# The lower half of the second network's first group moves from VectorE to GpSimd, and the token numbers of all units are turned on the third bank

## The chip, the cores and the metric

The kernel runs on one core of one Trainium2 chip. The metric is device time in microseconds (us), lower is better. A core has five engines with a queue each: TensorE (PE, its weight loads are PEld), VectorE (DVE), ScalarE (ACT), GpSimd (POOL) and SyncE (SP, which here only issues transfers). They meet through semaphores alone. PE writes into eight PSUM banks; DVE and ACT read those, and everything else that is spoken of lies in SBUF.

## The reference

Three steps follow each other, all in float32. Only the third is touched in its order of work, and the second in one detail:

```python
x = _attn_ref(q, k, v)            # banded attention, 2 x 768 tokens of 512
x = _moe_ref(x, w_gate, w1, w2)   # one expert of eight for each token, capacity 384
h = x @ w_in                      # 1536 x 512 by 512 x 2048
g = np.where(h > 0, h, np.exp(np.minimum(h, 0)) - 1)
out = g @ w_out                   # 1536 x 2048 by 2048 x 512
```

## The kernel before

Products are made in a fast 32-bit matmul form from halves: each float32 operand is rounded to an upper half (`h` in a name), and the rest is the lower half (`l`), subtracted from the operand. A product is then three matmuls: upper by upper, lower by upper, upper by lower.

**Experts.** The routed tokens are worked in units of 384 tokens of one expert. At the start of a unit `split_x` (L246) turns the unit's rows: first a small matmul (L250) turns the token numbers into a corner of a PSUM bank, ACT copies them out (L251, tile `it`), and then the four quarters of the rows are transposed into banks 0, 5, 6 and 7 in turn (L255, three transposes each), rounded by ACT (L256) and their lower halves subtracted by DVE (L257). In the first unit the token numbers go to the third of the banks listed, in the later ones to the second, bank 5. A bank that still has to be read isn't written, so that transposes into the bank of the token numbers wait for L251. Here a first unit and two later ones run.

**Second network.** The 1536 rows are worked in four groups of 384. `group(g)` (L1432) goes through 16 tiles f of 128 features. In each:

- PE makes the 12 matmuls of `hidden` (L241) into one of four PSUM banks in rotation;
- ACT makes three activations of it (L1450 to L1452);
- DVE makes four dependent instructions (L1465 to L1468) that turn these into the activated block x; the last one reads PSUM and one SBUF operand, the other three read two SBUF operands;
- the block is halved into `hh` and `hl`, tiles of a ring of four (HH): in group 0 ACT rounds the block of the tile before (`round_g`, L1425) and DVE subtracts its lower half (`rest_g`, L1429); in the later groups DVE does both (L1474, L1429);
- PE multiplies with w_out, three tiles late (LAG): `second_2` (L1401) makes nine matmuls for tile f - 3, and among its first three stand one that reads the lower half of w_out and one that reads `hl`.

In group 0 both weight matrices are halved on the way, in pieces of two tiles: `split_a2` for w_in and `split_b2` for w_out, ACT rounding and DVE subtracting (L1381). Also there, DVE finishes the last conversion of w_out (L419, L422, L412, tiles 3 to 5) and four subtractions for the next group's rows (L1361, tiles 6 to 12). The order on each engine is the order in which the code is written (the schedule is made by hand), so `rest_g(f - 1)` stands on DVE behind tile f's four instructions and, at odd f, behind `split_b2`. POOL has nothing to do in group 0; its next work there is the scattered put of group 0's rows (L1413) in group 1.

Of the kernel before, what the change touches and what calls it, by code (L numbers as in the profile page):

```python
# [9 lines left out]
F32 = mybir.dt.float32  # L10
# [6 lines left out]
ALU = mybir.AluOpType  # L17
# [11 lines left out]
P = 128  # L29
# [6 lines left out]
SLOT = 384  # L36
NS = SLOT // P
# [57 lines left out]
def moe_chain_kernel(  # L95
# [14 lines left out]
    nc = tc.nc  # L110
# [47 lines left out]
    at, _ = nc.bump_sbuf(4 * KD * FF)  # L158
# [10 lines left out]
    at, _ = nc.bump_sbuf(4 * FF // P * DM)  # L169
# [57 lines left out]
    XROW0 = wout[:, 0:4, :].rearrange("p a d -> p (a d)")[:, 0 : NS * ROW].rearrange("p (s d) -> p s d", s=NS)  # L227
# [18 lines left out]
    def split_x(xrow, hps, it):  # L246

        xh, xl = XS1
        at = hps[2 if xrow is XROW0 else 1][0:NS, SLOT : SLOT + P]
        nc.tensor.matmul(at, xrow[:, :, DM], ident, start=True, stop=True)  # L250
        nc.scalar.copy(IT[it], at)  # L251
        for kk in range(KD):
            xp = hps[kk % len(hps)][:, 0:SLOT]
            for s in range(NS):
                nc.tensor.transpose(xp[:, s * P : (s + 1) * P], xrow[:, s, kk * P : (kk + 1) * P], ident)  # L255
            nc.scalar.copy(xh[:, kk, :], xp)  # L256
            nc.vector.tensor_tensor(xl[:, kk, :], xp, xh[:, kk, :].bitcast(F32), op=ALU.subtract)  # L257
            yield
# [111 lines left out]
    def conv_load(i, after=()):  # L370
        half = NCHUNK // 2
        for n in range(2):
            if i < half:
                part, kk = divmod(i + n, KD)
                src = w_in[kk * P : (kk + 1) * P, part * CE : (part + 1) * CE]
            else:
                src = w_out[(i + n - half) * P : (i + n - half + 1) * P, :]
            ld = nc.sync.dma_start(raw_pair(i)[:, n * CE : (n + 1) * CE], src).ins
            for rows in after if n == 0 else ():
                tc.add_manual_dep(  # L380
                    ld,
                    rows.name,
                    mybir.DependencyInfo(mybir.DependencyClass.Sync, mybir.DependencyReason.DATA),
                    reason="the first unit's rows go first",
                )
# [49 lines left out]
    with ExitStack() as att:  # L435
# [549 lines left out]
        for n in range(NST - 1):  # L985
            at = lambda lag: steps[n - lag] if 0 <= n - lag < NST else None
# [35 lines left out]
        def counts():  # L1022
# [87 lines left out]
            op=ALU.mult,  # L1110
# [36 lines left out]
    def listed(n, j):  # L1147
        return lists_i[:, n * MAXU + j : n * MAXU + j + 1]
# [5 lines left out]
    def hidden(wa, jj, xa):  # L1154
        hp = new_hp()
        for _ in layer1(hp, wa, jj, xa):
            pass
        return hp
# [40 lines left out]
    def prologue(j, n):  # L1199

        if n == 0:
            split_a(0, W1_RAW[0])
        elif n == 1:
            for _ in split_x(XROW, HP[1:] + HP[:1], j % 2):
                pass

    def branch_ahead(label, hint):

        engines = [e.engine for e in (nc.tensor, nc.vector, nc.scalar, nc.gpsimd, nc.sync)]
        tc.mark_branch_hint_location(label, hint=hint, engines=engines)  # L1210
# [142 lines left out]
    def load_y(g, at):  # L1353
        nc.sync.dma_start(YR, ydT[:, ds(at, SLOT)].rearrange("(k p) n -> p k n", p=P))
        nc.sync.dma_start(IDT[g % 3], ids[ds(at, SLOT), :].rearrange("(s p) o -> p (s o)", p=P))

    def split_y(g, parts):
        yh, yl = YS[g % 2]
        for kk in parts:
            nc.scalar.copy(yh[:, kk, :], YR[:, kk, :])  # L1360
            nc.vector.tensor_tensor(yl[:, kk, :], YR[:, kk, :], yh[:, kk, :].bitcast(F32), op=ALU.subtract)  # L1361
# [21 lines left out]
    def split_a2(c):  # L1383
        split_2(AW[c], half_part(IN, c))

    def split_b2(c):
        split_2(BW[c], OUT[c])
# [4 lines left out]
    RINGS = [HF + slots[0:2], slots[2:4]]  # L1392
# [3 lines left out]
    def second_2(f, s):  # L1396
        c, jj = divmod(f, 2)
        cols = slice(s * P, (s + 1) * P)
        ga, wb = HH[f % 4], BW[c]
        for n, (a, b) in enumerate(((0, 0), (0, 1), (1, 0))):  # L1400
            nc.tensor.matmul(  # L1401
                ACC[s],
                ga[a][:, cols],
                wb[b][:, jj, :],
                start=(f == n == 0),
                stop=(f == NF2 - 1 and n == 2),
            )

    def take_out(g, s):
        nc.scalar.copy(OBS[(NS * g + s) % len(OBS)], ACC[s])  # L1410

    def put_out(g, s):
        put = nc.gpsimd.indirect_dma_start(  # L1413
            out,
            bass.IndirectOffsetOnAxis(ap=IDT[g % 3][:, s : s + 1], axis=0),
            OBS[(NS * g + s) % len(OBS)],
            None,
            bounds_check=NT - 1,
            oob_is_err=False,
        ).ins  # L1420
        tc.declare_no_dep(put, group="out", reason="no two rows have one token")
        tc.add_to_no_dep_group("out", put)

    def round_g(f):
        nc.scalar.copy(HH[f % 4][0], RINGS[0][f % 4])  # L1425

    def rest_g(f):
        gh, gl = HH[f % 4]
        nc.vector.tensor_tensor(gl, RINGS[0][f % 4], gh.bitcast(F32), op=ALU.subtract)  # L1429

    def group(g, tail):

        more = g + 1 < NG
        if g == 0:
            conv_load(NCHUNK - CONV_LATE)
        for f in range(NF2):
            c, jj = divmod(f, 2)
            if g == f == 0:
                split_b2(0)
            if g == 0 and f < LAG:  # L1440
                tail(f)
            if more and f == HINT_AT:
                branch_ahead(f"groups{g}", n_rows > (g + 1) * SLOT)
            hp = hidden(AW[c], jj, YS[g % 2])
            if g == 0 and jj == 0 and c + 1 < NC2:
                split_a2(c + 1)


            x, z = RINGS[0][f % 4], RINGS[1][f % 2]
            nc.scalar.activation(x, hp, AF.Relu, scale=-1.0)  # L1450
            nc.scalar.activation(z, x, AF.Tanh, scale=-0.5)  # L1451
            nc.scalar.activation(x, x, AF.Exp, scale=-1.0)  # L1452
            if f >= LAG:
                for s in range(NS):
                    second_2(f - LAG, s)
            elif g:
                for s in range(NS):
                    second_2(NF2 - LAG + f, s)
                    if f == LAG - 1:
                        take_out(g - 1, s)  # L1460
            if more and f == (0 if g else LAG - 1):
                load_y(g + 1, nc.sync.value_load(listed(NLIST - 1, 3 + g), min_val=0, max_val=NT - SLOT))
            if g == 0 and f:
                round_g(f - 1)
            nc.vector.scalar_tensor_tensor(z, x, 1.0, z, op0=ALU.add, op1=ALU.mult)  # L1465
            nc.vector.tensor_tensor(x, z, x, op=ALU.subtract)  # L1466
            nc.vector.scalar_tensor_tensor(x, x, 3.0, z, op0=ALU.add, op1=ALU.mult)  # L1467
            nc.vector.scalar_tensor_tensor(x, x, 0.5, hp, op0=ALU.mult, op1=ALU.max)  # L1468
            if g == 0 and jj and c:
                split_b2(c)  # L1470
            if g == 0 and f:
                rest_g(f - 1)
            if g or f == NF2 - 1:
                nc.vector.tensor_copy(HH[f % 4][0], x)  # L1474
                rest_g(f)
            if g == 0:
                lo, hi = (min(max(n - LATE_FROM, 0) * LATE_STEPS, len(late)) for n in (f, f + 1))
                for step in late[lo:hi]:
                    step()
            if g and f in PUTS:  # L1480
                put_out(g - 1, PUTS.index(f))
            if g == 0 and 2 <= f < 2 + NG:

                m = f - 2
                nc.sync.dma_start(
                    out[m * SLOT : (m + 1) * SLOT, :].rearrange("(s p) d -> p s d", p=P),
                    fill_row[:, 0:DM].unsqueeze(1).to_broadcast([P, NS, DM]),
                )
            if more and 6 <= f < 14 and jj == 0:
                split_y(g + 1, [(f - 6) // 2])  # L1490
# [14 lines left out]
    def groups(g, tail=None):  # L1505
        group(g, tail)
        if g + 1 < NG:
            with tc.If(n_rows > (g + 1) * SLOT, label=f"groups{g}") as more:
                groups(g + 1)
            with more.Else():  # L1510
                last_products(g)
        else:
            last_products(g)
# [4 lines left out]
    with tc.If(n_rows <= 2 * SLOT, label="rows"):  # L1518


        at = nc.sync.value_load(last_i[:, 0:1], min_val=0, max_val=NT)
# [52 lines left out]
```

## Time and profile before

| | us |
|---|---|
| median of three timed runs | 414.65 (414.61 to 416.39) |
| the profiled execution, its own time | 416.77 |
| its span from the first to the last instruction | 414.8 |
| PE busy | 396.7 (96%) |
| DVE busy | 335.1 (81%) |
| ACT busy | 236.2 (57%) |
| POOL busy | 65.0 (16%) |

The span has three stretches: attention and routing up to about 110 us, the expert units to about 205 us, and the four groups of the second network from there to the end, at about 67 us each. The granted clock of TensorE is 0.996 of full speed as a mean.

In the timeline's rows below the columns are start, duration (both us), engine, line, operation, output and inputs, shape, count, and in brackets the idle time just before and what ended it. Rows of four matmuls of a kind are merged into one row, whose start is that of the first.

### The profile page before, as it was taken

How to read it: one execution, taken by the hardware profiler on the slowest of the kernel's cores; microseconds unless marked ns; L12 is line 12 of the kernel's file. 1: busy time of each engine (PE TensorE's matmuls, PEld its weight loads, DVE VectorE, ACT ScalarE, POOL GpSimd, SP SyncE). 2: the span in 40 equal slices, each digit the busy share in tenths (PEclk: the TensorE clock that was granted, in tenths of full speed). 3: DMA queues.
4: the chain of work that ended last, by engine and by line, in shares of the span. 5: the costliest groups of instructions: out<-in, count | busy, mean ns of one | idle time of the engine just before them, and what ended most of it. 6: DMA issues, size and time to landing. Idle time of an engine off the chain costs nothing.

```text
span 414.8 us, 7899 instructions
## 1 busy us (share of the span) xinstructions
PE 396.7 (96%) x2736; PEld 346.8 (84%) x2736; DVE 335.1 (81%) x675; ACT 236.2 (57%) x588; POOL 65.0 (16%) x127
## 2 busy tenths in 40 slices
PE   7898999989999999999999999999999999999994
PEld 4586677668998989999889789998989898989883
DVE  6779788677589989878889999997788777778871
ACT  4887698673565738437586677635343425253421
POOL 5134876553100000000000000002000003000002
PEclk9999999999999999999999999999999999999998
DMA  8999998699576787995477000202000201000002
GB/s 258 274 278 270 283 286 255 184 348 316 186 250 226 245 292 260 349 285 186 158 241 304 0 2 0 78 0 77 0 0 2 77 2 50 26 2 0 2 2 77
DMA packets 33691, 63.60 MB, mean 153 GB/s; under 512 B 5302, under 2 KB 16191, under 8 KB 33642
## 3 DMA queue, kind: packets, MB, share of 16 engines
q1 hardware_dynamic: 31962, 58.28, 45.3%
q0 software_dynamic: 1680, 4.73, 3.1%
q8 instruction: 23, 0.38, 0.4%
q14 instruction: 26, 0.21, 0.1%
HBM read 50.19 MB, written 13.40 MB: 153 GB/s over the span
## 4 chain that ended last, share of the span: by engine, by line
PE 27%; issue 14%; DVE 6%; DMA 1%; POOL 1%; ACT 1%; another core or an unknown queue 0%; POOLq 0%; DVEq 0%
PE bank L241 14%; PE bank L1401 14%; DVE xrow L1465 1%; DMA raw<-in_moe_w_out_dram 1%; DVE win_r L1381 1%; DVE hl L1429 1%; POOL out_dram L1413 1%; DVE wout_r L1381 1%; DVE cst L1467 1%; DVE cst L1466 1%; DVE xrow L1466 0%; DVE xrow L1467 0%; DVE wout L412 0%; DVE wout L422 0%; ACT xrow L1451 0%
## 5 line engine op out<-in xcount | busy, mean ns | idle before, releaser
L1401 PE MATMUL bank<-wout_r,hh 128*128 128x512 f32 x144 | 56.5, 393 | 0.0
L640 ACT ACTIVATE ex<-bank,nm 128x120 f32<-128x120 f32 x96 | 33.5, 369 | 8.1 <-DVE nm L627 7.7
L1450 ACT ACTIVATE cst<-bank 128x384 f32<-128x384 f32 x24 | 11.8, 490 | 38.8 <-PE bank L241 38.8
L1450 ACT ACTIVATE xrow<-bank 128x384 f32<-128x384 f32 x24 | 11.8, 490 | 38.4 <-PE bank L241 38.2
L1401 PEld LDWEIGHTS bank<-wout_r,hh 128*128 128x128 f32 x144 | 27.1, 188 | 4.6 <-DVE wout_r L1381 0.3
L1413 POOL DMA_INDIRECT out_dram<-ysb,idt x3 | 2.9, 976 | 175.9 <-DVE xrow L1466 175.3
L1401 PE MATMUL bank<-w2raw_r,hl 128*128 128x512 f32 x72 | 28.8, 399 | 1.2 <-DVE hl L1429 1.2
L1401 PE MATMUL bank<-w2raw_r,hh 128*128 128x512 f32 x72 | 28.2, 392 | 0.0
L241 PE MATMUL bank<-yh,win_r 128*128 128x384 f32 x128 | 27.0, 338 | 0.0
L615 PE MATMUL bank<-kw,half 128*64 128x120 f32 x384 | 24.8, 271 | 1.9 <-DMA half<-in_q_dram 1.1
L615 PEld LDWEIGHTS bank<-kw,half 128*64 128x64 f32 x384 | 19.8, 136 | 6.2 <-issue 3.8
L1413 POOL DMA_INDIRECT out_dram<-raw,idt x6 | 6.1, 1024 | 119.3 <-ACT raw L1410 118.1
L241 PE MATMUL bank<-xh,wal 128*128 128x384 f32 x104 | 22.9, 341 | 0.9 <-DVE wal L234 0.9
L241 PEld LDWEIGHTS bank<-yh,win_r 128*128 128x128 f32 x128 | 22.8, 188 | 0.3
L1465 DVE SCALAR_TENSOR_TENSOR xrow<-xrow 128x384 f32<-128x384 f32 x24 | 13.4, 557 | 9.3 <-ACT xrow L1452 8.6
L275 PE MATMUL bank<-hh,wbh_r 128*128 128x384 f32 x96 | 20.8, 337 | 0.0
L275 PE MATMUL bank<-hl,wbh_r 128*128 128x384 f32 x96 | 20.6, 336 | 0.0
L640 ACT ACTIVATION_READ_ACCUMULATOR ex<-bank,nm 128x1 f32 x96 | 20.5, 214 | 0.0
L1465 DVE SCALAR_TENSOR_TENSOR xrow<-cst,xrow 128x384 f32<-128x384 f32 x24 | 13.3, 556 | 8.5 <-ACT cst L1452 8.5
L241 PEld LDWEIGHTS bank<-xh,wal 128*128 128x128 f32 x104 | 18.1, 188 | 2.5 <-DVE wal L234 2.2
L1401 PEld LDWEIGHTS bank<-w2raw_r,hl 128*128 128x128 f32 x72 | 13.5, 188 | 5.5 <-DVE hl L1429 2.6
L269 ACT ACTIVATE xrow<-xrow,gate 128x512 f32<-128x512 f32 x9 | 6.5, 722 | 20.1 <-DVE gate L264 15.9
(287 smaller groups left out, 1116.1 us busy)
## 6 DMA issues: line engine op xcount, KB each, us to landing
raw<-in_moe_w_out_dram SPq DMA_DIRECT2D x16, 512.0 KB
w1raw<-in_moe_w_dram SPq DMA_DIRECT2D x12, 512.0 KB
w2raw<-in_moe_w_dram SPq DMA_DIRECT2D x12, 512.0 KB
raw<-in_moe_w_in_dram SPq DMA_DIRECT2D x10, 512.0 KB
half<-in_q_dram SPq DMA_DIRECT2D x24, 128.0 KB
w2raw<-in_v_dram SPq DMA_DIRECT2D x6, 512.0 KB
rows<-in_moe_w_in_dram SPq DMA_DIRECT2D x6, 512.0 KB
yr<-ydT SPq DMA_DIRECT2D x4, 768.0 KB
```

What stands on the lines that cost most here:

```text
L241: nc.tensor.matmul(hp, wa[a][:, kk, cols], xa[b][:, kk, :], start=(n == kk == 0), stop=(n == 2 and kk == KD - 1))
L269: nc.scalar.activation(xrow[:, s, 0:DM], xrow[:, s, 0:DM], AF.Copy, scale=GATE[:, s : s + 1])
L275: nc.tensor.matmul(ACC[d][:, 0:SLOT], wb[a][:, jj, d * P : (d + 1) * P], hb[b], start=(f == 0 and n == 0), stop=(f == NF1 - 1 and n == 2),)
L615: nc.tensor.matmul(sp[cols, u, :], qts[i][:, g, u, cols], kws[i][:, g, u, j, :], start=True, stop=True)
L640: nc.scalar.activation(ex[:, u, :], sp[:, u, :], AF.Exp, bias=nm[:, u : u + 1], accum_out=dens[i][:, g, u])
L1381: nc.vector.tensor_tensor(lo, src, hi.bitcast(F32), op=ALU.subtract)
L1401: nc.tensor.matmul(ACC[s], ga[a][:, cols], wb[b][:, jj, :], start=(f == n == 0), stop=(f == NF2 - 1 and n == 2),)
L1413: put = nc.gpsimd.indirect_dma_start(out, bass.IndirectOffsetOnAxis(ap=IDT[g % 3][:, s : s + 1], axis=0), OBS[(NS * g + s) % len(OBS)], No ...
L1429: nc.vector.tensor_tensor(gl, RINGS[0][f % 4], gh.bitcast(F32), op=ALU.subtract)
L1450: nc.scalar.activation(x, hp, AF.Relu, scale=-1.0)
L1465: nc.vector.scalar_tensor_tensor(z, x, 1.0, z, op0=ALU.add, op1=ALU.mult)
L1466: nc.vector.tensor_tensor(x, z, x, op=ALU.subtract)
```

## The change

```diff
@@ split_x
-        at = hps[2 if xrow is XROW0 else 1][0:NS, SLOT : SLOT + P]
+        at = hps[2][0:NS, SLOT : SLOT + P]
@@
-    def rest_g(f):
+    def rest_g(f, engine=nc.vector):
         gh, gl = HH[f % 4]
-        nc.vector.tensor_tensor(gl, RINGS[0][f % 4], gh.bitcast(F32), op=ALU.subtract)
+        engine.tensor_tensor(gl, RINGS[0][f % 4], gh.bitcast(F32), op=ALU.subtract)
@@ group
             if g == 0 and f:
-                rest_g(f - 1)
+                rest_g(f - 1, nc.gpsimd)
```

Fifteen subtractions, those of tiles 0 to 14 of group 0, go from DVE's queue to POOL's. The one of tile 15 and those of the later groups stay on DVE. In the later units the token numbers are turned into bank 6 instead of bank 5.

On DVE, in group 0 at tile 1 (`cst` and `xrow` are the rings of blocks, `hl0` the lower half of tile 0, `win1` the second quarter of w_in), a line with a minus stands only in the kernel before:

```order
 L1467 SCALAR_TENSOR_TENSOR cst_66<-cst_66,xrow_1892 128x384
 L1468 SCALAR_TENSOR_TENSOR cst_66<-cst_66,bank5_89 128x384
-L1429 TENSOR_TENSOR hl0_152<-cst_66,hh0_151 128x384
 L1381 TENSOR_TENSOR win1_r_97<-win1_96,wal1_143 128x4x256
 L1465 SCALAR_TENSOR_TENSOR xrow_1892<-xrow_1892 128x384
```

The subtraction is gone, and the next piece of w_in follows the tile's last instruction at once. On POOL, from the branch into the second network on:

```order
 L1518 COMPARE_AND_BRANCH
 L1518 UNCONDITIONAL_BRANCH x2
-L1210 REGISTER_ALU
-L1570 BRANCH_PREFETCH_HINT
+L1429 TENSOR_TENSOR hl0_152<-cst_66,hh0_151 128x384
+L1429 TENSOR_TENSOR hl1_154<-cst_66,hh1_153 128x384
+L1429 TENSOR_TENSOR hl2_156<-xrow_1892,hh2_155 128x384
+L1429 TENSOR_TENSOR hl3_1901<-xrow_1892,hh3_1900 128x384
```

Eleven more like these follow, around the branch hint, and then the puts of group 1 as before; between the fifteen POOL has no other work. On PE, at the start of a later unit (`xrow` are the unit's rows, `cst` holds the identity):

```order
 L275 MATMUL bank4_88<-hh1_153,wbh0_r_145 128x384
-L250 MATMUL bank5_89<-cst_66,xrow_1892 3x128
+L250 MATMUL bank6_90<-cst_66,xrow_1892 3x128
 L255 MATMUL bank0_84<-cst_66,xrow_1892 128x128 x3
 L255 MATMUL bank5_89<-cst_66,xrow_1892 128x128 x3
```

The matmul keeps its place and writes the bank that the transposes reach third instead of second.

## Rows read from the trace of the kernel before

**Rows 1.** Busy time in two stretches of group 0: PE, PEld, DVE, ACT, POOL, clock, DMA
```profile
210.48:237.65 27.17, 26.02 (x130) 22.84 (x128) 26.44 (x43) 18.64 (x35) 0.00 (x0) 1.00 0.47 165
243.01:259.34 16.33, 16.33 (x84) 14.87 (x83) 15.91 (x27) 12.03 (x22) 0.00 (x0) 1.00 0.00 1
```

**Rows 2.** Chain that ended last, by time: start, us, what
```profile
237.09 0.56 DVE hl L1429
...
237.70 1.90 PE bank L1401 x7
...
348.54 2.10 PE bank L241 x12
```

**Rows 3.** Timeline of PE: first matmuls of tiles 3, 4, 8, 10, 12; one of tile 15
```profile
212.19 0.85 PE L241 MATMUL bank<-yh,wah 128*128 128x384 f32 x4
...
217.30 0.87 PE L241 MATMUL bank<-yh,wal 128*128 128x384 f32 x4
...
234.43 0.87 PE L241 MATMUL bank<-yh,w1raw_r 128*128 128x384 f32 x4
...
243.74 0.87 PE L241 MATMUL bank<-yh,w1raw_r 128*128 128x384 f32 x4
...
252.11 0.87 PE L241 MATMUL bank<-yh,w1raw_r 128*128 128x384 f32 x4
...
266.97 0.39 PE L1401 MATMUL bank<-wout_r,hh 128*128 128x512 f32 x1
```

**Rows 4.** Timeline of DVE: two tiles of group 0, and a later piece of w_out
```profile
241.40 0.55 DVE L1429 TENSOR_TENSOR hl<-xrow,hh 128x384 fp32r<-128x384 f32 x1
241.87 1.22 DVE L1381 TENSOR_TENSOR win_r<-win,w1raw_r 128x1024 fp32r<-128x1024 f32 x1
243.01 0.55 DVE L1465 SCALAR_TENSOR_TENSOR xrow<-cst,xrow 128x384 f32<-128x384 f32 x1
...
251.17 0.55 DVE L1465 SCALAR_TENSOR_TENSOR xrow<-xrow 128x384 f32<-128x384 f32 x1
...
264.77 1.22 DVE L1381 TENSOR_TENSOR wout_r<-wout,wbh_r 128x1024 fp32r<-128x1024 f32 x1
```

**Rows 5.** Instructions of POOL by line: count, shortest/median/longest ns, first and last start
```profile
L567 POOL TENSOR_TENSOR w2raw<-w2raw x12: 453/460/589, 35.2 to 43.6; 128x128 f32<-128x128 f32 x12
L926 POOL TENSOR_TENSOR wal<-w1raw,wah_r x4: 717/724/742, 61.2 to 74.2; 128x256 fp32r<-128x256 f32 x4
L764 POOL TENSOR_SCALAR idx<-row,ob x9: 294/299/1279, 38.2 to 93.8; 128x1 uint32<-128x1 f32 x9
```

**Rows 6.** Timeline of DVE and POOL where both read SBUF, or one alone
```profile
33.26 0.29 DVE L514 TENSOR_SCALAR kw<-rows 64x384 f32<-64x384 f32 x1
...
40.57 0.32 DVE L514 TENSOR_SCALAR kw<-rows 64x320 f32<-64x320 f32 x1
...
42.61 0.54 POOL L567 TENSOR_TENSOR w2raw<-w2raw 128x128 f32<-128x128 f32 x1
42.76 0.61 DVE L514 TENSOR_SCALAR kw<-rows 64x384 f32<-64x384 f32 x1
...
75.67 0.88 POOL L926 TENSOR_TENSOR wal<-w1raw,wah 128x256 fp32r<-128x256 f32 x1
75.90 0.84 DVE L514 TENSOR_SCALAR kw<-rows 64x320 f32<-64x320 f32 x1
...
93.66 1.23 DVE L422 SCALAR_TENSOR_TENSOR win<-raw,win 128x1024 uint32<-128x1024 uint32 x1
93.77 1.28 POOL L764 TENSOR_SCALAR idx<-row,ob 128x1 uint32<-128x1 f32 x1
```

**Rows 7.** Timeline of PE: the transposes of the two later units
```profile
125.52 0.55 PE L255 MATMUL bank<-cst,xrow 128*128 128x128 f32 x3
126.58 1.20 PE L255 MATMUL bank<-cst,xrow 128*128 128x128 f32 x9 [0.51 <-ACT it L251]
...
162.88 1.62 PE L255 MATMUL bank<-cst,xrow 128*128 128x128 f32 x12
```

## The prediction

> **What bounds the kernel now.** I read the chain of waits first, then busy time by stretch, then the timelines of PE and DVE in group 0 of the second network, where the moved instructions stand, and last the places where POOL and DVE work at the same time. The chain [rows 2] ends in a long run of matmuls, from 237.70 us to the last group, without a wait in it: whatever is lost or won before 237.7 us, or by a new wait in group 0, is carried to the end. Just ahead of that run stands a DVE instruction, the subtraction of `hl` that the change moves. So from the start of group 0 to 237.65 us DVE sets the pace, and after that PE. The busy times say how narrowly: DVE is busy 26.44 of 27.17 us in the first stretch and 15.91 of 16.33 us in the second [rows 1], and what is missing are the short hops between its dependent steps; PE is without work only in the first stretch. POOL is idle in both. The clock is 1.00, the 2.4 GHz level, in both, so the short waits of PE there cost nothing beyond themselves.
>
> How much PE loses in group 0 can be read from the starts of its tiles [rows 3]. Two tiles take 252.11 - 243.74 = 8.37 us where PE never waits. From tile 3 to 4 it takes 217.30 - 212.19 = 5.11 us where half of 8.37, 4.19, would do: 0.92 lost. From tile 4 to 8 it takes 17.13 us against 16.74: 0.39. From tile 8 to 10 9.31 against 8.37: 0.94. Together 2.25 us. That is all that a faster DVE could give back here.
>
> DVE needs 251.17 - 243.01 = 8.16 us for two tiles in the even part [rows 4], against PE's 8.37. The two engines are level to 0.21 us in two tiles, which is what makes the change delicate in both directions.
>
> **The change part by part.** *What leaves DVE.* One subtraction takes 241.87 - 241.40 = 0.47 us of DVE's time from start to start [rows 4], the 0.55 us of its row less the overlap with the next. Two tiles would take 8.16 - 0.94 = 7.22 us. Nothing else on DVE waits for `hl`; PE does, and the buffers' next users.
>
> *What POOL needs.* No subtraction of 384 columns by POOL is in the trace. Those of 128 and 256 columns take at least 0.453 and 0.717 us [rows 5]; continued by the same step of 0.264 that is an estimate of 0.98 us. POOL has nothing else to do, and a tile takes PE 4.19 us, so POOL itself keeps up. The path of one `hl`, too, is longer only by half a microsecond and begins earlier, since it waits only for ACT's rounding and no longer for whatever DVE has in front; PE wants it two tiles later. Behind these instructions on POOL stand only each other, the branch hint, and the puts of group 1, which start after all of them.
>
> *What it does to DVE.* Here the rows speak against the change. At 93.66 us DVE begins a step of 1.23 us with two SBUF operands, and a POOL instruction of 128x1 that starts at 93.77 takes 1.28 us where its median is 0.299 [rows 5, 6]: it ends 0.16 us after DVE's. The other way round, a DVE instruction that starts at 75.90 inside a POOL subtraction (75.67 to 76.55) takes 0.84 us, against 0.32 for the same shape alone at 40.57; it ends 0.19 us after POOL's. And one at 42.76, inside a POOL subtraction that ends at 43.15, takes 0.61 against 0.29 alone at 33.26 [rows 6]. So the one that has begun to read holds the other off until it is done, and POOL, when it waits, gets in before DVE's next instruction (the one at 75.90 came directly behind another of DVE's). The two DVE instructions that were held have one SBUF operand; that those with two are held too is inferred from the first case, in which one of them did the holding. In group 0 three of the four steps of a tile, both weight splits and the splits of the rows have two SBUF operands; only L1468, with one operand in PSUM, might run beside POOL.
>
> The Trainium skill (SBUF — State Buffer, "Who interferes with whom") says for this what no row here shows: a VectorE instruction with two SBUF inputs contends with a GpSimd instruction that reads SBUF, and the loser is blocked for the whole instruction. By that rule the forecast below stands and the rival without sharing falls.
>
> *The price of one held DVE step.* The two cases give 0.84 - 0.32 = 0.52 us behind a POOL subtraction of 256 columns and 0.61 - 0.29 = 0.32 us behind one of 128. That is 0.13 to 0.20 us less than the shortest time of the POOL instruction itself. For 384 columns: by the step from the one to the other 0.72, by 0.98 less 0.13 0.85; the bounds are 0 (DVE isn't held at all) and 0.98 (held for all of it). I take 0.80, in the middle of the two that come from rows.
>
> *The sum in group 0.* DVE then takes 7.22 + 2 x 0.80 = 8.82 us for two tiles, more than PE's 8.37, so DVE sets the pace through the whole of group 0. The last instruction of DVE on which PE depends closely is the piece of w_out for tiles 12 and 13: it ends at 264.77 + 1.22 = 265.99, and PE reads it at 266.97 [rows 3, 4], 0.98 us to spare. (The piece behind it is used in group 1, where DVE has time.) Ahead of it on DVE stand 12 of the moved subtractions, tiles 0 to 11, in a stretch in which DVE was never idle. It comes later by 12 x (0.80 - 0.47) = 3.96 us, and PE by 3.96 - 0.98 = 2.98 us. That includes what the removed waits for `hl` give: they turn into waits for the halves of the weights. From there PE runs through to the end.
>
> *The token numbers.* In the first of the two later units PE waits 0.51 us for ACT's copy of them before it may transpose into bank 5 [rows 7]. With bank 6 three more transposes go ahead of that wait; twelve take 1.62 us, so about 0.12 us each, and 3 x 0.12 = 0.36 of the 0.51 us is filled. In the second there is no such wait. Bank 6 is free in both. I take 0.3 us off, with bounds of 0 (a later wait takes it back, since ACT ends no sooner) and 0.5.
>
> Together +2.98 - 0.3 = +2.7 us. The profiled execution took 416.77 us with a span of 414.8; its span would become 417.5 and its own time 419.5. The median of the runs shown, 414.65, lies 2.1 below the profiled one; the change adds the same to it: 417.3 us.
>
> **The rivals.** *No sharing worth the name* (the faster side): DVE's two-operand steps aren't held by POOL, or for less than the 0.47 us that each saves. The place is tiles 2 to 5 of group 0, the price PE's 2.25 us of waits, and it decides below a price of 0.47 + (0.98 + 0.3) / 12 = 0.58 us for each held step. With no holding at all: 414.65 - 2.25 - 0.3 = 412.1 us. For it: no row shows a two-operand DVE step being held. Against it: POOL is held by such a step for its whole length, and what keeps two readers apart in one direction should do so in the other.
>
> *POOL only gets in beside L1468.* DVE's steps follow each other within 0.03 us, and POOL may lose each time until the step that reads PSUM. Then 0.80 less the 0.47 us from L1468's start to the next, 0.33 us, is paid where 0.47 is saved: DVE gains 12 x 0.14 = 1.7 us, most of PE's waits go, and the time is about 412.7 us. Against it: at 75.90 POOL was let in between two DVE instructions.
>
> *The two cancel.* Some of the held steps fall where DVE would have waited anyway, or a held step is paid with about 0.55 us: within half a microsecond of 414.4 us.
>
> *DVE is held for all of POOL's instruction, or POOL's is longer.* At 0.98 us: 12 x 0.51 - 0.98 - 0.3 = +4.8, 419.5 us; at 1.1 us, since POOL's instructions are themselves held and lengthen (0.88 us at 75.67 against 0.72), +6.3, 420.9 us.
>
> **How the numbers follow.** The forecast, prices of 0.72 to 0.97 us, has 0.50 of the chance and a range of its own of 416.4 to 419.4 us (12 x 0.25 - 0.98 - 0.3 = +1.7 to the upper end just given). Full holding or more has 0.10, cancelling 0.13, POOL beside L1468 0.12, no sharing 0.15. Half a per cent, about what a measurement of this kernel can tell from no change, is 2.07 us: below 412.6 or above 416.7. Faster: no sharing almost whole and half of POOL beside L1468, 0.19. Slower: all of the longer holding and 0.43 of the forecast, 0.53. The rest, 0.28, is within. For 8 in 10 the range reaches from 412.0, which leaves out the better half of no sharing, to 420.0, which leaves out the longest holding.
>
> **What would show it.** In the profile after: L1429 on POOL with a mean of about 1 us or more, fifteen times; DVE's two-operand steps in group 0 (L1465 to L1467, L1381) longer than the 0.55 and 1.22 us of now, by about 0.8 us once per tile; L1468 unchanged; PE's first matmul of tile 12 some 3 us later than 252.11, and its waits no longer for `hl` but for the lower halves of weights (`win_r`, `wout_r`, L1381). The forecast is wrong if these DVE steps keep their durations and DVE shows idle time; then PE has no wait in group 0 and the time is near 412. It is wrong in size if the held steps cost other than 0.8 us. For the token numbers: PE's wait before L255 at 126.6 us falls from 0.51 to about 0.15 us.

## The result and the profile after

The changed kernel takes 419.68 us (median of 11 runs, 417.79 to 422.25) where the kernel before took 415.88 beside it (11 runs, 414.28 to 417.35): a ratio of 1.0089, 95% interval 1.0062 to 1.0116. On 415.9 us that is 3.7 us more, between 2.6 and 4.8. The profiled execution took 419.82 us with a span of 417.9, against 414.8 for the span before.

Only three of the four groups run with these inputs: the trace before has 48 subtractions of `hl`, 16 to a group. Behind group 0 stand two groups of about 67 us each.

**POOL and DVE.** First the fifteen subtractions on POOL by line: count, shortest/median/longest ns, first and last start.

```profile
L1429 POOL TENSOR_TENSOR hl<-cst,hh x8: 1132/1327/2079, 212.8 to 269.2; 128x384 fp32r<-128x384 f32 x8
L1429 POOL TENSOR_TENSOR hl<-xrow,hh x7: 1134/1258/2080, 220.0 to 273.4; 128x384 fp32r<-128x384 f32 x7
```

They are there, in the place named, and last 1.13 to 2.08 us. The timeline of POOL in two tiles shows why so unevenly (start, duration, engine, line, operation; in brackets the idle time before and what ended it):

```profile
239.54 1.14 POOL L1429 TENSOR_TENSOR hl<-xrow,hh 128x384 fp32r<-128x384 f32 x1 [5.14 <-issue]
243.34 2.08 POOL L1429 TENSOR_TENSOR hl<-xrow,hh 128x384 fp32r<-128x384 f32 x1 [2.66 <-ACT hh L1425]
```

And the timeline of DVE around them, with the first step two tiles later and the last piece of w_out, which answers to [rows 4]:

```profile
239.25 0.55 DVE L1465 SCALAR_TENSOR_TENSOR xrow<-xrow 128x384 f32<-128x384 f32 x1
239.83 1.26 DVE L1466 TENSOR_TENSOR xrow<-xrow 128x384 f32<-128x384 f32 x1
241.13 0.56 DVE L1467 SCALAR_TENSOR_TENSOR xrow<-xrow 128x384 f32<-128x384 f32 x1
241.72 0.56 DVE L1468 SCALAR_TENSOR_TENSOR xrow<-xrow,bank 128x384 f32<-128x384 f32 x1
242.19 1.22 DVE L1381 TENSOR_TENSOR wout_r<-wout,w2raw_r 128x1024 fp32r<-128x1024 f32 x1
243.32 1.22 DVE L1381 TENSOR_TENSOR win_r<-win,w1raw_r 128x1024 fp32r<-128x1024 f32 x1
244.46 1.38 DVE L1465 SCALAR_TENSOR_TENSOR xrow<-cst,xrow 128x384 f32<-128x384 f32 x1
...
253.21 1.37 DVE L1465 SCALAR_TENSOR_TENSOR xrow<-xrow 128x384 f32<-128x384 f32 x1
...
268.43 1.22 DVE L1381 TENSOR_TENSOR wout_r<-wout,wbh_r 128x1024 fp32r<-128x1024 f32 x1
```

Read the two together. POOL starts at 243.34, two hundredths of a microsecond after a weight split of DVE. That split keeps its 1.22 us and ends at 244.54; POOL's row ends at 245.42, 0.88 us behind it. The next DVE step starts at 244.46 and takes 1.38 us instead of 0.55: it ends at 245.84, 0.42 us after POOL. At 239.54 the same happens on a smaller scale: POOL begins inside L1465, which ends at 239.80, is done 0.88 us later at 240.68, and L1466, begun at 239.83, takes 1.26 instead of 0.56 and ends 0.41 us after POOL. So each subtraction on POOL first waits for the DVE step that is reading, then holds the next one: one two-operand step of DVE per tile is lengthened, by 0.70 where it depends on the step before it (L1466, L1467) and by 0.82 where it doesn't and its row starts earlier. L1468, which reads PSUM, keeps 0.55 to 0.56. Two tiles take DVE 253.21 - 244.46 = 8.75 us, against 8.16 before.

Busy time in four tiles of the even part answers to the second of [rows 1] (PE, PEld, DVE, ACT, POOL, clock, DMA):

```profile
244.46:261.95 17.49, 17.23 (x85) 15.05 (x84) 17.07 (x23) 12.20 (x23) 6.42 (x5) 1.00 0.00 0
```

The same four tiles took 16.33 us before, with DVE busy 15.91. Four DVE instructions fewer (23 against 27), and yet 1.16 us more busy time: a count of instructions would have said the opposite. DVE's share of the time is 98% here, and a busy row doesn't tell whether the engine works or is held.

**PE.** What PE waits for in group 0 (total us, times, longest):

```profile
PE bank L1401 <- DVE wout_r L1381: 3.1, 3, 1.5
PE bank L241 <- DVEq L1518: 0.3, 1, 0.3
PE bank L241 <- DVE win_r L1381: 0.3, 1, 0.3
```

In the kernel before the list has, beside the same wait for DVE's queue:

```profile
PE bank L1401 <- DVE hl L1429: 1.2, 2, 0.7
```

The two waits for `hl` on DVE, the second of which led into the long run [rows 2], are gone, and waits for the lower halves of the weights stand there instead. In the timeline of PE (the first row is the token edit's place, the others answer to [rows 3]):

```profile
124.99 0.87 PE L255 MATMUL bank<-cst,xrow 128*128 128x128 f32 x6 [0.18 <-ACT it L251]
...
204.85 0.86 PE L241 MATMUL bank<-yh,wah_r 128*128 128x384 f32 x4
...
207.51 0.85 PE L241 MATMUL bank<-yh,wah_r 128*128 128x384 f32 x4
...
233.58 0.50 PE L1401 MATMUL bank<-wout_r,hh 128*128 128x512 f32 x1 [1.49 <-DVE wout_r L1381]
...
243.46 0.49 PE L1401 MATMUL bank<-wout_r,hh 128*128 128x512 f32 x1 [0.70 <-DVE wout_r L1381]
...
254.16 0.87 PE L241 MATMUL bank<-yh,w1raw_r 128*128 128x384 f32 x4
...
269.71 0.50 PE L1401 MATMUL bank<-wout_r,hh 128*128 128x512 f32 x1
...
271.65 0.87 PE L241 MATMUL bank<-xh,wah_r 128*128 128x384 f32 x4
```

204.85 is the first matmul of group 0 (205.51 before), 254.16 the first of tile 12 (252.11), 269.71 the one that needs the last critical piece of w_out (266.97), 271.65 the first of group 1 (268.80 before). From the group's start to its use of that piece PE takes 64.86 us against 61.46: 3.40 more. DVE's piece ends at 269.65, 0.06 us ahead of PE's use; before there were 0.98 us to spare. DVE's first L1465 of the group is this row in the kernel before, and the next one in the kernel after; from there to the end of the piece it takes 265.99 - 210.48 = 55.51 us before and 59.83 after:

```profile
210.48 0.56 DVE L1465 SCALAR_TENSOR_TENSOR xrow<-cst,xrow 128x384 f32<-128x384 f32 x1 [0.28 <-ACT cst L1452]
```

```profile
209.82 0.56 DVE L1465 SCALAR_TENSOR_TENSOR xrow<-cst,xrow 128x384 f32<-128x384 f32 x1 [0.28 <-ACT cst L1452]
```

The chain says the same (start, us, what):

```profile
266.07 1.27 DVE cst L1466
267.37 0.57 DVE cst L1467
267.96 0.55 DVE cst L1468
268.51 1.15 DVE wout_r L1381
269.71 2.11 PE bank L1401 x8
```

PE's run without a wait now begins at 269.71, not at 237.70 [rows 2]. DVE's share of the whole chain rose from 6% to 13%, PE's fell from 27% to 20%.

### The profile page after: what moved, and what is told of

Same layout as the page of the kernel before. It is cut to its first block, busy times and chain, and to the rows that moved or that the text cites. A ratio compares the mean times of both kernels' runs of the same rounds, so it can differ in the third digit from the quotient of the medians.

```text
span 417.9 us, 7926 instructions
## 1 busy us (share of the span) xinstructions
PE 397.2 (95%) x2736; PEld 346.3 (83%) x2736; DVE 340.0 (81%) x660; ACT 235.1 (56%) x588; POOL 85.4 (20%) x142
## 3 DMA queue, kind: packets, MB, share of 16 engines
q1 hardware_dynamic: 31962, 58.28, 45.1%
## 4 chain that ended last, share of the span: by engine, by line
PE 20%; issue 15%; DVE 13%; ACT 1%; DMA 1%; POOL 1%; another core or an unknown queue 0%; POOLq 0%; DVEq 0%
PE bank L241 10%; PE bank L1401 10%; DVE xrow L1465 3%; DVE win_r L1381 2%; DVE wout_r L1381 2%; DVE cst L1466 1%; DVE cst L1467 1%; DVE xrow L1466 1%; DMA raw<-in_moe_w_out_dram 1%; POOL out_dram L1413 1%; DVE xrow L1467 1%; DVE xl L1361 1%; DVE wout L412 0%; DVE cst L1468 0%; DVE xrow L1468 0%
## 5 line engine op out<-in xcount | busy, mean ns | idle before, releaser
L1429 POOL TENSOR_TENSOR hl<-cst,hh 128x384 fp32r<-128x384 f32 x8 | 11.0, 1379 | 126.5 <-ACT hh L1425 126.5
L1465 DVE SCALAR_TENSOR_TENSOR xrow<-cst,xrow 128x384 f32<-128x384 f32 x24 | 15.8, 658 | 8.6 <-ACT cst L1452 8.6
L1465 DVE SCALAR_TENSOR_TENSOR xrow<-xrow 128x384 f32<-128x384 f32 x24 | 15.8, 658 | 8.3 <-ACT xrow L1452 8.2
L627 DVE TENSOR_REDUCE nm<-bank 128x4 f32<-128x480 f32 x24 | 15.6, 651 | 2.1 <-PE bank L615 1.8
```

Of the source, the lines that this page charges most:

```text
L627: nc.vector.tensor_reduce(nm, sp, axis=AX.X, op=ALU.max, negate=True)
L1429: engine.tensor_tensor(gl, RINGS[0][f % 4], gh.bitcast(F32), op=ALU.subtract)
```

## The experiments

Theory: a subtraction on POOL holds one two-operand step of DVE that is longer held than the subtraction cost DVE; the sum of these prices ahead of the last critical piece of w_out is the loss. Rivals: the token edit costs it; PE waits for a late `hl` from POOL; it is POOL's writing, or its being busy at all, that holds DVE.

One wait disturbs comparisons: ahead of its second block of matmuls in group 0 PE waits for DVE's queue to pass the branch (DVEq L1518 or its like), between 0.16 and 1.42 us from one profile to the next. The first figure of the table starts behind it, at the first matmul of tile 1, and ends at the first of group 1. But DVE isn't put off by as much as PE, so a long wait gives it a head start: its first L1465 stands 2.45 us behind tile 1's first matmul before, 2.31 after, and 1.84 to 2.02 us in the runs with waits of 0.62 to 1.42 us. The second figure therefore starts at that L1465; where DVE sets the pace it is the one to go by, and where PE does, the gain of the edit lies between the two.

| kernel | tile 1 to group 1, us | less before | first L1465 to group 1, us | less before | time, ratio to before |
|---|---|---|---|---|---|
| before | 268.80 - 208.03 = 60.77 | | 268.80 - 210.48 = 58.32 | | 1 |
| after | 271.65 - 207.51 = 64.14 | +3.37 | 61.83 | +3.51 | 1.0089 [1.0062, 1.0116] |
| token edit alone | 60.73 | -0.04 | 58.28 | -0.04 | 1.0012 [0.9989, 1.0035] |
| POOL alone | 63.73 | +2.96 | 61.89 | +3.57 | 1.0102 [1.0057, 1.0147] |
| beside L1468 | 61.37 | +0.60 | 59.35 | +1.03 | 1.0043 [1.0018, 1.0068] |
| late conversion | 58.85 | -1.92 | 56.91 | -1.41 | 0.9966 [0.9940, 0.9991] |
| POOL reads | 67.65 | +6.88 | 65.81 | +7.49 | 1.0193 [1.0143, 1.0242] |
| POOL writes | 60.14 | -0.63 | 58.30 | -0.02 | 0.9998 [0.9968, 1.0028] |
| late conversion, early `hl` | 58.40 | -2.37 | 56.56 | -1.76 | 0.9950 [0.9925, 0.9974] |

**The token numbers alone.** The kernel before with

```diff
-        at = hps[2 if xrow is XROW0 else 1][0:NS, SLOT : SLOT + P]
+        at = hps[2][0:NS, SLOT : SLOT + P]
```

> The kernel before with the second edit alone: the token numbers of all units are turned on the third bank. Sharing theory (all of the loss comes from the moved subtractions): the wait ahead of the transposes in the first later unit falls from 0.51 to 0.18 us, the twelve transposes of the second take 1.53 instead of 1.62 us, group 0 of the second network keeps its 63.3 us from its first matmul to the first of group 1, and the time is 0 to 0.5 us below before, which the timing can't tell from no change. Rival (the token edit has a part in the loss, since PE waited 0.9 us more for expert weights after it in the changed kernel's profile): the time is 0.5 to 1 us above before and those waits of PE (on L233 and L234, 100 to 206 us) are again at about 2.7 instead of 1.3 us.

PE's row at the first later unit:

```profile
127.98 0.87 PE L255 MATMUL bank<-cst,xrow 128*128 128x128 f32 x6 [0.20 <-ACT it L251]
```

The wait is 0.20 us where it was 0.51 [rows 7], as in the kernel after (0.18). The time shows neither gain nor loss, and group 0 is that of the kernel before: the loss there isn't the token edit's. Whether this half of the change gives 0.3 us isn't shown, since the interval reaches from 0.5 us less to 1.5 us more. PE's waits for expert weights behind it (L233, L234), which the rival named, are 2.0 us here, 1.3 before, 2.7 after and 1.5 in the next run, without this edit; one profile of each doesn't tell whether the edit moves them.

**The subtractions alone.** The kernel before with the two hunks at `rest_g` and no other:

```diff
-                rest_g(f - 1)
+                rest_g(f - 1, nc.gpsimd)
```

> The kernel before with the first edit alone: fifteen subtractions of group 0 on POOL. Sharing theory: group 0 takes 66.8 us from its first matmul to the first of group 1, as in the changed kernel, against 63.3 before; thirteen DVE steps ahead of the w_out piece of tiles 12 and 13 are longer by 0.7 to 0.82 us; the time is 3.4 us above before (ratio 1.008). Rival (token edit): less than 2.5 us above before.

PE's waits in group 0:

```profile
PE bank L1401 <- DVE wout_r L1381: 2.7, 3, 1.5
PE bank L241 <- DVEq L1518: 1.0, 1, 1.0
PE bank L241 <- DVE win_r L1381: 0.3, 1, 0.3
```

The same waits as after, for the same pieces, and the whole of the loss: 3.57 us from DVE's first step, against 3.51, and the intervals of the two ratios overlap.

**POOL made to start beside the step that reads PSUM.** The kernel after, with each subtraction on POOL also waiting for the third DVE step of the next tile:

```diff
-        engine.tensor_tensor(gl, RINGS[0][f % 4], gh.bitcast(F32), op=ALU.subtract)
+        ins = engine.tensor_tensor(gl, RINGS[0][f % 4], gh.bitcast(F32), op=ALU.subtract).ins
+        if engine is nc.gpsimd:
+            tc.add_manual_dep(ins, third[f + 1], ...)
...
-            nc.vector.scalar_tensor_tensor(x, x, 3.0, z, op0=ALU.add, op1=ALU.mult)
+            step3 = nc.vector.scalar_tensor_tensor(x, x, 3.0, z, op0=ALU.add, op1=ALU.mult)
+            if g == 0:
+                third[f] = step3.ins.name
```

> The changed kernel, with each of the fifteen subtractions on POOL waiting also for the third step of the next tile on DVE (L1467), so that it begins together with L1468, which reads PSUM and one SBUF operand. No work is added; the lower halves come later by up to a tile. Sharing theory (only steps with two SBUF operands are held): L1468 keeps its 0.55 us, the step behind it is longer by about 0.4 instead of 0.7 to 0.82 us, two tiles of DVE take about 8.1 us instead of 8.75, and the time lies 1.5 to 2.5 us below the changed kernel, that is 1 to 2 us above before or level with it. Rival (POOL holds every DVE instruction that touches SBUF): L1468 is longer by about 0.9 us and the time stays at the changed kernel's. Second rival (the loss comes from lower halves that arrive late at PE): later halves make it slower than the changed kernel, above 1.010 of before, with PE waiting for hl.

POOL by line, then its timeline at one tile, then DVE there (L1479 is L1468 of the other kernels, L1431 the subtraction):

```profile
L1431 POOL TENSOR_TENSOR hl<-cst,hh x8: 1010/1020/1027, 213.8 to 268.6; 128x384 fp32r<-128x384 f32 x8
```

```profile
244.79 1.02 POOL L1431 TENSOR_TENSOR hl<-xrow,hh 128x384 fp32r<-128x384 f32 x1 [4.04 <-DVE cst L1476]
```

```profile
240.07 1.76 DVE L1381 TENSOR_TENSOR wout_r<-wout,w2raw_r 128x1024 fp32r<-128x1024 f32 x1
...
244.65 0.56 DVE L1479 SCALAR_TENSOR_TENSOR cst<-cst,bank 128x384 f32<-128x384 f32 x1
245.12 1.10 DVE L1361 TENSOR_TENSOR xl<-yr,xh 128x384 fp32r<-128x384 f32 x1
```

Now POOL is not held: fifteen times 1.01 to 1.03 us. It runs beside L1479, which keeps its 0.56 us: a step with one operand in PSUM isn't in its way. But POOL goes on into the next step, which has two operands and is held by 0.54 to 0.55 us in the even part (1.10 for 0.55, 1.76 for 1.22), and by up to 0.68 ahead of it. I had expected 0.4, since I had left out that POOL starts 0.14 us behind L1479. Two tiles take 8.33 us, 0.42 less than after, and the time falls by about 2 us, from 1.0089 to 1.0043. The edit has a second effect, though: the lower halves come later. PE's waits in group 0, beside the one at the branch:

```profile
PE bank L1401 <- POOL hl L1431: 0.9, 2, 0.5
PE bank L1401 <- DVE wout_r L1381: 0.8, 1, 0.8
```

The waits for `wout_r` fall from 3.1 to 0.8 us, and 0.9 us of waiting for POOL's `hl` is new. So a smaller price goes with a smaller loss, and later halves did not make the kernel slower than after; what the smaller price alone would give isn't shown. The kernel is still slower than before. The last of these waits ends at 237.55 us, and in the even part behind it DVE's 8.33 us are within PE's 8.37; but DVE itself gains nothing from the move, since 0.55 is more than the 0.47 that the subtraction costs there.

**POOL reads, DVE keeps its work.** The kernel before, `hl` on DVE, and a POOL subtraction into a tile that nobody uses:

```diff
+    SPARE = rh.tile([P, 368], F32, name="spare")
...
                 rest_g(f - 1)
+                hh = HH[(f - 1) % 4][0].bitcast(F32)[:, 0:368]
+                nc.gpsimd.tensor_tensor(SPARE, hh, hh, op=ALU.subtract)
```

> The kernel before, with hl still on DVE, and a subtraction on POOL added in tiles 1 to 15 of group 0: 368 columns of the rounded block (hh) from itself into a tile that nobody reads, started by the same rounding of ACT as in the changed kernel. Nobody waits for its result. Sharing theory: each holds one DVE step with two SBUF operands for 0.7 to 0.8 us; the thirteen that fall ahead of the w_out piece of tiles 12 and 13 make it 9 to 10 us later, less the 0.98 us to spare, so group 0 takes 71 to 72.5 us instead of 63.3 and the time is 8 to 9 us above before (ratio 1.019 to 1.022). Rival (the changed kernel lost because lower halves came late from POOL): no POOL result is on PE's path, so group 0 keeps its 63.3 us and the time is level with before.

POOL and DVE at one of its instructions, and PE's waits in group 0 (lines are one higher than before):

```profile
242.93 1.03 POOL L1475 TENSOR_TENSOR spare<-hh 128x368 f32<-128x368 f32 x1 [2.95 <-ACT hh L1426]
```

```profile
242.09 1.22 DVE L1382 TENSOR_TENSOR wout_r<-wout,w2raw_r 128x1024 fp32r<-128x1024 f32 x1
243.22 1.15 DVE L1430 TENSOR_TENSOR hl<-xrow,hh 128x384 fp32r<-128x384 f32 x1
```

```profile
PE bank L1402 <- DVE hl L1430: 4.0, 7, 0.6
PE bank L1402 <- DVE wout_r L1382: 1.3, 3, 0.9
PE bank L241 <- DVEq L1521: 0.9, 1, 0.9
```

Nobody waits for POOL's result here, and the kernel loses 8 us (ratio 1.0193), 7.5 of them between DVE's first step and group 1. DVE's own subtraction, 0.55 us alone, takes 1.15. A late `hl` from POOL is therefore not needed for a loss, and after shows only one such wait, 0.2 us of PE's weight load. The price here, 0.48 to 0.61 us, is below that of after and below the 0.7 to 0.8 that I had expected: POOL, here with both operands from the same tile, ends 0.65 us behind the DVE step it waited for (243.96 less 243.31), where it took 0.88 in the kernel after. Why it is quicker was not tried. The whole group took 70.88 us, a little less than the 71 to 72.5 expected.

**POOL writes only.** The same with three memsets of that tile instead, the first behind ACT's rounding:

```diff
+                for n in range(3):
+                    put = nc.gpsimd.memset(SPARE, 0.0).ins
...
```

> As e5_read, but POOL only writes: in place of each added subtraction three fills of the same spare tile with zeros (368 columns each, about 0.35 us), together about as long. Sharing theory (it is the reading of SBUF by POOL that holds DVE's second operand): DVE's steps keep 0.56 and 1.22 us, group 0 keeps 63.3 us and the time is level with before within 0.4 per cent. Rival (any POOL instruction on SBUF holds them): DVE steps are longer by 0.3 to 1 us per tile and the time is as in e5_read, or at least 4 us above before.

POOL, then DVE beside it (L1468 and L1469 are L1465 and L1466 of before):

```profile
245.92 1.34 POOL L1477 MEMSET spare<- 128x368 f32 x3 [3.03 <-ACT hh L1428]
```

```profile
246.11 0.55 DVE L1468 SCALAR_TENSOR_TENSOR xrow<-cst,xrow 128x384 f32<-128x384 f32 x1
246.70 0.56 DVE L1469 TENSOR_TENSOR cst<-xrow,cst 128x384 f32<-128x384 f32 x1
```

1.34 us of writing per tile beside two-operand steps, and these keep 0.55 and 0.56 us. The ratio is 0.9998. So it is POOL's reading that holds DVE; neither its writing nor its being busy does. The Trainium skill (SBUF — State Buffer, "Who interferes with whom") says so too: a GpSimd instruction that only writes isn't in the way of a two-input VectorE instruction, one that reads is. Both halves agree with these two runs.

**The gain without POOL.** What the change could have won, PE's 2.25 us of waits, can be sought on DVE itself. The last conversion of w_out, three steps of 2.9 us in tiles 3 to 5, isn't needed until later:

```diff
-    LATE_FROM = 3
+    LATE_FROM = 12
```

> The kernel before with one number changed: the three steps of the last conversion on DVE (2.9 us in all) go from tiles 3 to 5 of group 0 to tiles 12 to 14, behind the pieces of the weights that PE waits for. Nothing goes to POOL. Theory that DVE's work ahead of those pieces sets the pace of group 0: PE's waits at tiles 4 to 10 (0.39 and 0.94 us) vanish, the one for the first lower half (0.9 us) stays, group 0 takes 61.7 to 62.2 us instead of 63.3, and the time is 1.2 to 1.6 us below before (ratio 0.996 to 0.997, about at the bound of what timing tells). Rival (group 0's pace comes from ACT or from the products' order): no change in group 0's 63.3 us.

PE's last wait for `hl` in group 0:

```profile
214.87 0.50 PE L1401 MATMUL bank<-w2raw_r,hl 128*128 128x512 f32 x1 [0.17 <-DVE hl L1429]
```

The second of the two waits of 1.2 us in all is gone with the conversion, and the kernel is faster than before, 0.9966 [0.9940, 0.9991]. The first wait is 0.17 us where it was 0.68; that isn't the edit's, since the wait at the branch, 0.69 us here, gives DVE a head start of 0.51 us. The wait that is left is for the first `hl`, so the next version keeps the late conversion, takes that subtraction between the second and third step of tile 1, and has the token edit as well:

```diff
+            if g == 0 and f == 1:
+                rest_g(0)
...
-            if g == 0 and f:
+            if g == 0 and f > 1:
                 rest_g(f - 1)
```

> A version meant to beat both: the kernel before with the token numbers on the third bank, the last conversion's three steps in tiles 12 to 14 (as in e4_late), and the first lower half (tile 0) subtracted by DVE between the second and third step of tile 1 instead of behind the fourth. Nothing goes to POOL. Theory that DVE's order and work ahead of PE's next operand set the pace of group 0: PE's last wait there (0.9 us before tile 0's third product) goes as well, group 0 takes 61 to 61.5 us (63.3 before, 61.9 in e4_late), and the time is 2 to 2.6 us below before, ratio 0.994 to 0.995. Rival (DVE has no slack in tile 1 either): the wait comes back at the next weight piece and group 0 takes 61.9 us as in e4_late.

DVE at tile 1 (L1469 is L1467 of before), and all of PE's waits in group 0:

```profile
212.93 0.56 DVE L1466 TENSOR_TENSOR cst<-xrow,cst 128x384 f32<-128x384 f32 x1
213.41 0.55 DVE L1429 TENSOR_TENSOR hl<-cst,hh 128x384 fp32r<-128x384 f32 x1
213.88 0.55 DVE L1469 SCALAR_TENSOR_TENSOR cst<-cst,xrow 128x384 f32<-128x384 f32 x1
```

```profile
PE bank L241 <- DVEq L1520: 1.4, 1, 1.4
```

413.28 us where before takes 415.23 beside it, a ratio of 0.9950 [0.9925, 0.9974]: it beats the kernel before, and with it the one after. From tile 1 on PE never waits, so 58.40 us is what PE needs there, and the 2.37 us less are the waits of the kernel before that were read as 2.25 from the tiles' starts. Not all of them went by the edits: 0.61 us of head start came from the wait at the branch, and from DVE's first step the gain is 1.76 us. Whether the early `hl` adds to the late conversion isn't shown, since the intervals of the two ratios overlap. My figure for the whole group, 61 to 61.5 us, was missed: it took 266.65 - 204.47 = 62.18, since the wait at the branch was 1.42 us in this execution. What sets the wait at the branch was not tried.

## Why the prediction was right, and where its sizes were off

The forecast was 2.7 us more, from holding that costs more than the move saves. 3.7 were measured, with 2.7 inside the interval. Step by step:

- *What leaves DVE*: 0.47 us per subtraction. Right; twelve of them leave ahead of the critical piece, 5.64 us.
- *What POOL needs*: an estimate of 0.98 us from the rows of 128 and 256 columns [rows 5]. It is 1.02 where it isn't held. That its row grows to 2.08 when it meets a weight split of DVE was not forecast, but POOL has the time and PE waited only 0.2 us for it.
- *Two-operand steps of DVE are held*: this was inferred from the other direction [rows 6] and carried the sign. Shown: by the rows of after, by the run in which POOL only reads (+8 us) and the one in which it only writes (nothing).
- *The price*: 0.80 us, from rows of shorter instructions. It is 7 times 0.82 and 6 times 0.70, a mean of 0.765. All the held steps of group 0, in the four runs that have them, follow one relation to 0.02 us: the held step ends its own duration less 0.14 us after POOL does, so that the price is POOL's end less the step's start less 0.14. At 244.46: 245.42 - 244.46 - 0.14 = 0.82. At 239.83: 0.71 against 0.70. Beside L1468: 245.81 - 245.12 - 0.14 = 0.55. In the run that only reads: 243.96 - 243.22 - 0.14 = 0.60. I had read the price off POOL's duration instead, and that is why one figure stood for what are two. That it lies so near their mean is in part luck.
- *How many*: 12 was one too few, and this is the term that was mis-sized most. On DVE the subtraction of tile 12 stood behind the last critical piece; on POOL nothing keeps it there, and it holds a step ahead of the piece, L1466 at 266.07. 13 prices are 7 x 0.82 + 6 x 0.70 = 9.94 us; less 5.64 that makes +4.30. Measured from DVE's first L1465 of the group to the end of that piece, 59.83 - 55.51 = +4.32 us.
- *To spare*: 0.98 us, of which 0.06 is left. 4.32 - 0.98 + 0.06 = 3.40, which is what PE lost up to there. With the prediction's own 12 and 0.80 it was 2.98.
- *Tile 12*: foretold some 3 us later than 252.11, found 2.05 later (2.71 counted from each group's start). The 3 us belong to the last piece, and at tile 12 not all of the prices have been paid.
- *The token numbers*: the wait fell to 0.18 us, near the 0.15 foretold. The 0.3 us didn't show: 1.0012 [0.9989, 1.0035] alone.
- *Two tiles on DVE*: 8.82 foretold, 8.75 measured. *L1468 unchanged*: right.

Of the rivals, *no sharing* and *the two cancel* are refuted by the held steps. *POOL only gets in beside L1468* is doubly out: POOL is let in between any two steps, and when it was made to start beside L1468, 0.14 us behind it, the price was 0.55, not 0.33, above the 0.47 saved. *DVE is held for all of POOL's instruction* is out as well: 0.70 to 0.82 us were paid, not 0.98. The measured 419.68 us looks like that rival's 419.5 only because the kernel before took 1.2 us more beside it than when the forecast was made (415.88 against 414.65).

The measured 3.7 us and the 3.4 of group 0 agree within the interval. The span's difference of 3.1 is the 3.5 between the first matmuls of groups 0 and 1, less 0.66 by which group 0 began earlier in this execution, and 0.25 behind it. That 0.66 isn't due to the token edit as far as the runs tell: with it alone, group 0 began at 207.21.

## What to carry to other kernels

Where VectorE runs two-operand steps back to back, as here, moving one to an idle GpSimd pays only if what GpSimd reads holds VectorE for less than the instruction cost there: here 0.70 to 0.82 us were paid for 0.47, and the engine with fewer instructions had more to do. Price it by GpSimd's end less the held step's start (less 0.14 us here), and count every instruction that now runs ahead of the critical one, also those that used to stand behind it. Where an engine is short of time in a few tiles only, look first for work on its own queue that can come later: moving three steps within DVE made this kernel 0.3% faster, the move to another engine 0.9% slower.

## What the runs showed of the hardware

- POOL, when it waits for a DVE step that is reading, gets in before DVE's next instruction even where the two stand back to back: 0.88 us from the end of DVE's row to the end of its own, against 1.02 us alone.
- The ends of POOL's rows can be used here: in three of the runs a held step of 128x384 ends 0.41 or 0.42 us after POOL's row. The Trainium skill (Perfetto Trace Analysis, "GPSIMD Engine Instruction") advises treating such spans as unreliable. For these instructions their length is indeed no measure of POOL's work, since it holds the wait for DVE (1.13 to 2.08 us against 1.02), but their ends are exact enough to work out a price.
- Memsets on POOL, 0.41 us each, leave DVE's two-operand steps beside them at 0.55 and 0.56 us, and a subtraction on POOL beside a DVE step with an operand in PSUM lasts 1.01 to 1.03 us while that step keeps its 0.55 to 0.56.
